# Bucketed attention and two MoE layers on one core: q and k loaded as one transposed tile per head

## The chip, the cores and the metric

The kernel runs on one core of a Trainium2 chip. The metric is device microseconds of one launch, median of 3 runs.

Words used below: TensorE (PE) does matmuls and transposes into PSUM, VectorE (DVE), ScalarE (ACT) and GpSimd (POOL) are the elementwise engines, and SP issues all DMAs of the kernel before. Each engine works through its own instructions in program order and waits at the first one whose inputs or buffers are not ready.

## The reference

There are 2 batches, 8 heads (16 head problems in all), 768 tokens and head dimension 64. All data are float32.

```
q_bits = (q @ proj) > 0 ; k_bits = (k @ proj) > 0        # proj is 64 x 6
bucket = sum(bits * 2**i)                                # 0..63 per token
scores = q @ k.T / 8 ; where(q_bucket != k_bucket, -1e9)
attn   = softmax(scores) (denominator + 1e-9) ; x = attn @ v
x      = heads side by side: 1536 x 512
h = x @ w_in1 ; x = (h * cos(h)) @ w_out1                # 512 -> 2048 -> 512
h = x @ w_in2 ; out = (h * tanh(softplus(h))) @ w_out2
```

## The kernel before

**Precision.** Matmuls run on values rounded to a reduced float32 form (float32r). To keep precision every operand is split into a high part (the rounded value) and a low part (the rest), and a product is the sum of high x high, high x low and low x high.

**Attention.** `attention()` first prepares head 0 in `first_head()`, then runs a loop over t with one *pass* for each block of 128 query rows: six passes (j = 0 to 5) per head. H1 counts the heads in this loop; the scores of head H1 are computed in passes j = 1 to 5 of H1 and j = 0 of the next. A pass issues, in this order: `fin` (U leaves PSUM and is moved to its place), `pt(c, 0)`, `qk(t)`, `exp(t-1)`, `pt(c, 1)`, `pv(c-1)`, then `norm`, a pending addition, one item from a GpSimd list (`gn`) and one piece of weight conversion (`fill`). c is t - 6, so transposing and multiplying with v runs six passes behind the scores. Four slots (0 to 3) inside a pass hold the preparation of the next heads: `plan` says which step goes where; (4, 3) is slot 3 of pass j = 4.

The steps and their names in the profile:

- `qk` (L326, tile s): the scores of 128 queries against 768 keys, two products of 128 contraction rows. Tiles q1 and k1 hold in rows 0 to 63 a one-hot code of the bucket (scaled so that tokens of other buckets fall away) and in rows 64 to 127 the high parts; q2 and k2 hold high and low parts. `s` has two buffers.
- `exp` (L335) writes p and its row sums; `norm` (L344 to L348) scales p by 1/sum, on GpSimd.
- `pt` (L363, wp): three transposes of p blocks; ScalarE copies the high part ph (L367), VectorE the low part pl (L369).
- `pv` (L379, u): four matmuls accumulating into U, which has one PSUM buffer and is copied out by ScalarE in passes j = 2 and 5 (L391, us); a DMA (sh) moves half of it to the other partitions and GpSimd adds both (L396), and every second head splits the result into xh and xl (L399, L402).

Preparing a head (the part that changes): q, k and v are loaded with tokens on partitions (rq, rk, rv, L249). On GpSimd `nat` makes high and low parts side by side (nq, nk, nv; L257, L259), one instruction per pass from the list `gn`. `setup_tr` (L277, wt) transposes three blocks and ScalarE evicts them, for q with the factor 1/8; four such units per head, at (4, 3) and (5, 3) of one head and (0, 1) and (0, 3) of the next. After the second unit of each side a DMA (L279) copies the high rows to q1 or k1. `setup_bits` (L287, wb) is four matmuls per half with proj split high and low, and the sign (L290, sg). `setup_mask` (L294 wm, L300 oh) compares with the 64 codes, and two DMAs (L304, L305) put the one-hot rows into q1 and k1.

The first head does the same steps by hand, with `keep_warm` matmuls (L435, ww) that compute nothing.

**MoE.** `moe()` runs 11 groups of matmuls h (L176) and o (L667) by an order written out in `runs`. While attention runs, four units of weights are already converted in small pieces (`fill`, L131 to L155), from t = 7 on for about eight heads.

Of the kernel before, what the change touches and what calls it, by code (L numbers as in the profile page):

```python
# [25 lines left out]
C_ID, C_CODE, C_SC = 0, 128, 256  # L26
# [3 lines left out]
def host_consts():  # L30
    c = np.zeros((128, NC_CONST), np.float32)
    c[:, C_ID:C_ID + 128] = np.eye(128, dtype=np.float32)
    code = 2.0 * (np.arange(64)[None, :] >> np.arange(6)[:, None] & 1) - 1.0
    c[0:6, C_CODE:C_CODE + 64] = code
    c[32:38, C_CODE + 64:C_CODE + 128] = -code
    c[:64, C_SC], c[64:, C_SC] = -BIG, 1.0
    c[:, C_SC + 1] = np.pi / 2
    c[:, C_SC + 2] = MAGIC
    c[:64, C_SC + 3], c[64:, C_SC + 3] = 5.0, -5.0
    c[:, C_SC + 4] = -1.2e-38  # L40
    c[:, C_SC + 5] = -5.0 * BIG
    return c


@with_exitstack
def lsh_moe_kernel(ctx: ExitStack, tc: tile.TileContext, q, k, v, proj, w_in1, w_out1, w_in2, w_out2, cst, out):
    nc = tc.nc
    B, H, S, D = q.shape
    J = S // 128
    DM = H * D  # L50
# [4 lines left out]
    SCALE = 1.0 / float(D) ** 0.5  # L55
# [18 lines left out]
    oh_s, half_pi, magic, oh_t, tiny, big5 = (con[:, C_SC + i:C_SC + i + 1] for i in range(6))  # L74
    ident_r = persist.tile([128, 128], F32R, name="ident_r")
    pr = persist.tile([128, 6], F32, name="pr")
    prw = persist.tile([128, 2, 128], F32, name="prw")
    prs = persist.tile([128, 2, 2, 128], F32R, name="prs")
# [146 lines left out]
    def attention():  # L225
        actx = ExitStack()
        with actx:
# [12 lines left out]
            NH = B * H  # L240
            rawt, natq, natk, natv = {}, {}, {}, {}
            tt = {}

            srcs = {"q": (q, nat_p, natq, 1), "k": (k, nat_p, natk, 0), "v": (v, v_p, natv, 0)}

            def load(nm, h):
                if h < NH:
                    t = rawt[nm, h] = nat_p.tile([128, J, D], F32, tag="r" + nm, name="r" + nm)
                    nc.sync.dma_start(out=t, in_=srcs[nm][0][h // H, h % H].rearrange("(p j) d -> p j d", j=J))  # L249

            def nat(nm, h):
                if h >= NH:
                    return
                _, pool, dst, hi = srcs[nm]
                r = rawt.pop((nm, h))
                n = dst[h] = pool.tile([128, J, 2, D], F32R, tag="n" + nm, name="n" + nm)
                nc.gpsimd.tensor_scalar(n[:, :, hi, :], r, 1.0, 1.0, ALU.mult, ALU.mult)  # L257
                yield
                nc.gpsimd.tensor_tensor(n[:, :, 1 - hi, :], r, f32(n[:, :, hi, :]), ALU.subtract)  # L259
                yield  # L260

            def tr_unit(n, half):
                w = ps_w.tile([128, HF], F32R, tag="w", name="wt")
                for j in range(3):
                    nc.tensor.transpose(  # L265
                        w[:, j * 128:j * 128 + 128], n[:, 3 * half + j].rearrange("p a d -> p (a d)"), ident_r
                    )
                return f32(w)

            def setup_tr(h, half, side):  # L270
                if half == 0 and side == 0:
                    tt[h] = {nm: t_p.tile([128, S], F32R, tag=nm, name=nm, bufs=2 + (nm[1] == "2")) for nm in ("q1", "q2", "k1", "k2")}
                    tt[h]["oh"] = oh_p.tile([128, S], F32R, tag="oh", name="oh")
                T = tt[h]
                nat_t, a, b, rows, sc = ((natq, "q2", "q1", 64, SCALE), (natk, "k2", "k1", 0, 1.0))[side]
                o = T[a][:, half * HF:half * HF + HF]
                nc.scalar.activation(o, tr_unit(nat_t[h], half), ACTF.Copy, scale=sc)  # L277
                if half == 1:
                    nc.sync.dma_start(out=f32(T[b][64:128, :]), in_=f32(T[a][rows:rows + 64, :]))  # L279
                    nat_t.pop(h)  # L280

            def setup_bits(h, half):
                T = tt[h]
                cs = slice(half * HF, half * HF + HF)
                w = ps_w.tile([128, HF], F32, tag="w", name="wb")
                for i, (x, nm, part) in enumerate((x, nm, part) for x, nm in enumerate(("q2", "k2")) for part in range(2)):
                    nc.tensor.matmul(w, prs[:, part, x, :], T[nm][:, cs], start=(i == 0), stop=(i == 3))  # L287
# [4 lines left out]
            def match(h, half):  # L292
                w = ps_w.tile([128, HF], F32, tag="w", name="wm")
                nc.tensor.matmul(w, code, tt[h]["sg"][:, half * HF:half * HF + HF])  # L294
                return w

            def setup_mask(h, half):
                T = tt[h]
                o = T["oh"]
                nc.vector.tensor_scalar(  # L300
                    o[:, half * HF:half * HF + HF], match(h, half), oh_t, oh_s, ALU.is_gt, ALU.mult
                )
                if half == 1:
                    nc.sync.dma_start(out=f32(T["q1"][0:64, :]), in_=f32(o[0:64, :]))  # L304
                    nc.sync.dma_start(out=f32(T["k1"][0:64, :]), in_=f32(o[64:128, :]))  # L305
# [13 lines left out]
            def qk(t):  # L319
# [4 lines left out]
                for n, (a, c) in enumerate((("q1", "k1"), ("q2", "k2"))[:: 1 if t else -1]):  # L324
# [13 lines left out]
            def norm(t):  # L338
                p, sm = P[t]
                s2 = sm_p.tile([128, 1], F32, tag="s2", name="s2")  # L340
                r = sm_p.tile([128, 1], F32, tag="r", name="r")

                def add():
                    nc.vector.tensor_scalar_add(s2, sm, 1e-9)  # L344

                def scale():
                    nc.vector.reciprocal(r, s2)
# [81 lines left out]
            nc.gpsimd.memset(prw, 0.0)  # L429
# [7 lines left out]
            def first_head():  # L437
                keep_warm(14)
                load("q", 0)
                load("k", 0)  # L440
                nc.sync.dma_start(out=con, in_=cst)
                nc.sync.dma_start(out=pr[0:64, :], in_=proj)
                nc.sync.dma_start(out=pr[64:128, :], in_=proj)
                for nm in "qk":
                    load(nm, 1)
                load("v", 0)
                n = {}
                for nm in "qk":
                    n[nm] = nat_p.tile([128, J, 2, D], F32R, tag="n" + nm, name="n" + nm)
                rq, rk = rawt.pop(("q", 0)), rawt.pop(("k", 0))  # L450
                nc.vector.tensor_copy(n["q"][:, :, 1, :], rq)
                nc.scalar.activation(n["k"][:, :, 0, :], rk, ACTF.Copy)
                nc.vector.tensor_tensor(n["q"][:, :, 0, :], rq, f32(n["q"][:, :, 1, :]), ALU.subtract)
                nc.gpsimd.tensor_copy(ident_r, ident)
                nc.vector.tensor_tensor(n["k"][:, :, 1, :], rk, f32(n["k"][:, :, 0, :]), ALU.subtract)
                nc.gpsimd.tensor_copy(prw[:, 0, 0:6], pr)
                nc.gpsimd.tensor_copy(prw[:, 1, 32:38], pr)
# [3 lines left out]
                T = tt[0] = {  # L461
                    nm: t_p.tile([128, S], F32R, tag=nm, name=nm, bufs=2 + (nm[1] == "2")) for nm in ("q1", "q2", "k1", "k2")
                }
                for half in range(2):
                    cs = slice(half * HF, half * HF + HF)
                    wq, wk = tr_unit(n["q"], half), tr_unit(n["k"], half)
                    nc.scalar.activation(T["q2"][:, cs], wq, ACTF.Copy, scale=SCALE)
                    nc.vector.tensor_copy(T["k2"][:, cs], wk)
                nc.sync.dma_start(out=f32(T["q1"][64:128, :]), in_=f32(T["q2"][64:128, :]))
                nc.sync.dma_start(out=f32(T["k1"][64:128, :]), in_=f32(T["k2"][0:64, :]))  # L470
                for nm in "qk":
                    load(nm, 2)
                for half in range(2):
                    setup_bits(0, half)
                keep_warm(6)
                for half in range(2):
                    cs = slice(half * HF, half * HF + HF)
                    w = match(0, half)
                    nc.scalar.activation(T["q1"][0:64, cs], w[0:64, :], ACTF.Relu, bias=big5[0:64, :], scale=BIG)
                    nc.vector.tensor_scalar(T["k1"][0:64, cs], w[64:128, :], -5.0, -1.0, ALU.is_gt, ALU.mult)  # L480
                load("v", 1)
                for nm, h in (("q", 1), ("k", 1), ("v", 0)):
                    drain(nat(nm, h))
# [34 lines left out]
            for t in range(-1, NT + LAG + 7):  # L518
# [3 lines left out]
                if H1 + 1 < NH:  # L522
                    h = H1 + 1
                    plan.update({
                        (0, 1): lambda: setup_tr(h, 1, 0), (0, 3): lambda: setup_tr(h, 1, 1),
# [207 lines left out]
```

## Time and profile before

| | us |
|---|---|
| median of 3 runs | 784.32 |
| lowest, highest | 783.73, 784.86 |
| profiled execution, span from first to last instruction | 782.2 |
| TensorE busy | 772.9 (99%) |
| VectorE busy | 516.7 (66%) |
| ScalarE busy | 500.9 (64%) |
| GpSimd busy | 221.8 (28%) |

The runs are timed around the launch, the profile from the first to the last instruction, so the time of a run is a little more than a span (2.1 us between the median and the span here). Shares are over the whole span; GpSimd works in the attention stage alone, the first third. The ends of matmuls are modelled, so TensorE's busy share is not its share of peak.

### The profile page before, as it was taken

The numbers are of one execution on the slowest core, as the hardware profiler recorded it, in microseconds if no ns is written. First come the engines' busy times: TensorE is split into PE (matmuls) and PEld (weight loads), VectorE is DVE, ScalarE is ACT, GpSimd is POOL, SyncE is SP. The second block draws the span as 40 slices with busy tenths as digits, with TensorE's granted clock in tenths as the row PEclk, the third lists the DMA queues.
The fourth block names the chain that finished last, engine by engine and source line by source line (L and its number), as shares of the span: only waits on it lengthen the run. The fifth ranks groups of instructions, "written<-read, shape, count | busy, mean of one in ns | idle before, by whom it ended". The sixth has DMA issues, their size and how long they took to land.

```text
span 782.2 us, 11575 instructions
## 1 busy us (share of the span) xinstructions
PE 772.9 (99%) x4020; PEld 662.4 (85%) x4020; DVE 516.7 (66%) x1004; ACT 500.9 (64%) x1002; POOL 221.8 (28%) x267
## 2 busy tenths in 40 slices
PE   8999999999999999999999999999999999999998
PEld 6889999999999788888888888888888888888886
DVE  5899899888997798578876437967213555521122
ACT  5999999998898797677776566955222534322120
POOL 6779999998886300000000000000000000000000
PEclk9999999999999999999999999999999999999999
DMA  5654454434220433113232002333101331000011
GB/s 168 184 149 109 107 147 126 107 99 121 71 67 16 118 109 107 54 54 108 90 99 81 0 1 82 108 108 100 35 1 35 101 106 57 0 23 32 0 54 54
DMA packets 38026, 62.35 MB, mean 80 GB/s; under 512 B 3664, under 2 KB 28368, under 8 KB 37968
## 3 DMA queue, kind: packets, MB, share of 16 engines
q1 hardware_dynamic: 37968, 61.63, 27.1%
q8 instruction: 31, 0.51, 0.3%
q14 instruction: 27, 0.22, 0.1%
HBM read 43.13 MB, written 3.15 MB: 59 GB/s over the span
## 4 chain that ended last, share of the span: by engine, by line
PE 95%; ACT 2%; DVE 1%; issue 1%; DMA 1%; SPq 0%; ACTq 0%
PE o L667 33%; PE h L176 32%; PE u L379 8%; PE s L326 8%; PE wp L363 8%; PE wb L287 3%; PE wt L265 2%; PE s L176 1%; PE wm L294 1%; PE ww L435 1%; DMA k<-oh 1%; DVE pa L643 0%; ACT ph L367 0%; ACT b L195 0%; ACT hs L335 0%
## 5 line engine op out<-in xcount | busy, mean ns | idle before, releaser
L176 PE MATMUL h<-xh,w 128*128 128x512 f32 x752 | 201.0, 389 | 0.0
L211 DVE TENSOR_TENSOR gl<-hs,gh 128x512 fp32r<-128x512 f32 x96 | 66.7, 695 | 192.6 <-ACT gh L209 192.4
L176 PEld LDWEIGHTS h<-xh,w 128*128 128x128 f32 x752 | 141.1, 188 | 29.3
L183 ACT ACTIVATE hs<-h 128x512 f32<-128x512 f32 x48 | 28.7, 598 | 163.2 <-PE h L176 163.2
L369 DVE TENSOR_TENSOR pl<-wp,ph 128x384 fp32r<-128x384 f32 x192 | 105.9, 552 | 23.4 <-ACT ph L367 22.9
L667 PE MATMUL o<-gh,w 128*128 128x512 f32 x384 | 118.3, 389 | 0.0
L667 PE MATMUL o<-w,gh 128*128 128x512 f32 x384 | 118.2, 389 | 0.0
L176 PE MATMUL h<-xl,w 128*128 128x512 f32 x376 | 115.9, 389 | 0.2 <-POOL xl L402 0.2
L367 ACT ACTIVATE ph<-wp 128x384 fp32r<-128x384 f32 x192 | 95.9, 500 | 17.4 <-PE wp L363 17.2
L326 PE MATMUL s<-k,q 128*128 128x512 f32 (+1 forms) x384 | 91.1, 359 | 3.2 <-DVE k L480 0.9
L328 DVE TENSOR_REDUCE nm<-s 128x1 f32<-128x768 f32 x96 | 90.1, 939 | 3.0 <-PE s L326 2.8
L667 PEld LDWEIGHTS o<-w,gh 128*128 128x128 f32 x384 | 72.1, 188 | 15.0
L667 PEld LDWEIGHTS o<-gh,w 128*128 128x128 f32 x384 | 72.0, 188 | 15.0 <-DVE pa L627 0.2
L176 PEld LDWEIGHTS h<-xl,w 128*128 128x128 f32 x376 | 70.5, 188 | 15.2 <-POOL xl L402 0.6
L667 PE MATMUL o<-gl,w 128*128 128x512 f32 x192 | 74.8, 390 | 0.2 <-DVE gl L211 0.2
L667 PE MATMUL o<-w,gl 128*128 128x512 f32 x192 | 74.7, 389 | 0.0
L379 PE MATMUL u<-ph,nv 128*128 128x384 f32 x192 | 72.6, 378 | 0.0
L186 ACT ACTIVATE hs<-h 128x512 f32<-128x512 f32 x46 | 27.5, 597 | 60.4 <-PE h L176 59.6
L326 PEld LDWEIGHTS s<-k,q 128*128 128x128 f32 x384 | 58.3, 189 | 8.5 <-DVE k L480 1.3
L379 PE MATMUL u<-pl,nv 128*128 128x384 f32 x192 | 64.9, 338 | 0.3 <-DVE pl L369 0.3
L209 ACT ACTIVATE gh<-hs 128x512 fp32r<-128x512 f32 x96 | 59.5, 620 | 1.6 <-PE o L667 1.4
L363 PE MATMUL wp<-con,hs 128*128 128x128 f32 x192 | 53.7, 280 | 0.0
(103 smaller groups left out, 1364.1 us busy)
## 6 DMA issues: line engine op xcount, KB each, us to landing
wr<-in_moe_w_in_dram SPq DMA_DIRECT2D x32, 512.0 KB, 3.8
wr<-in_moe_w_out_dram SPq DMA_DIRECT2D x32, 512.0 KB, 3.3
rq<-in_q_dram SPq DMA_DIRECT2D x16, 192.0 KB, 2.8
rk<-in_k_dram SPq DMA_DIRECT2D x16, 192.0 KB, 2.7
rv<-in_v_dram SPq DMA_DIRECT2D x16, 192.0 KB, 3.6
q<-q SPq DMA_DIRECT2D x16, 192.0 KB, 2.7
k<-k SPq DMA_DIRECT2D x16, 192.0 KB, 2.7
sh<-us SPq DMA_DIRECT2D x32, 96.0 KB, 2.3
```

The lines of the kernel that those rows point to most:

```text
L176: nc.tensor.matmul(hp, w[:, wi, c, :], X[b][c], start=(i == 0), stop=(i == 3 * NCT - 1))
L183: nc.scalar.activation(hs, hp, ACTF.Mish)
L186: nc.scalar.activation(hs, hp, ACTF.Copy, scale=INV2PI)
L209: nc.scalar.activation(gh, hs, ACTF.Copy)
L211: nc.vector.tensor_tensor(gl, hs, f32(gh), ALU.subtract)
L326: nc.tensor.matmul(s[:, c0:c1], T[a][:, qs], T[c][:, c0:c1], start=(n == 0), stop=(n == 1))
L328: nc.vector.tensor_reduce(nm, s, AX.X, ALU.max, negate=True)
L363: nc.tensor.transpose(w[:, j * 128:j * 128 + 128], P[h * J + 3 * half + j][:, kt * 128:kt * 128 + 128], ident)
L367: nc.scalar.activation(ph, w, ACTF.Copy)
L369: nc.vector.tensor_tensor(pl, w, f32(ph), ALU.subtract)
L379: nc.tensor.matmul(U[0], lw, x, start=(kt == 0 and n == 0), stop=(kt == J - 1 and n == 1))
L667: nc.tensor.matmul(O[d], lhs, rhs, start=(first and x == 0), stop=(last and x == 2))
```

## The change

The host now lays out, per head, one tile of 128 x 768: rows 0 to 63 are k transposed, rows 64 to 127 q transposed; v is laid out so that each partition reads one run, and proj is padded to 128 x 128 with its columns where the bits of q and k belong. In the kernel:

- one load of 128 x 768 per head takes the place of the loads of q and k; there are three buffers;
- no `nat` for q and k and no transposes. GpSimd multiplies the tile in place by a column that is 1 for k rows and 1/8 for q rows (`setup_scale`), ScalarE copies it to `hi` in one instruction (`setup_high`), GpSimd subtracts in two halves to get `lo` (`setup_low`);
- three DMAs copy k high to k1, q high and q low to q2 (`setup_moves`); after the hash bits one more overwrites the q rows of `lo` with k high, and after the mask two more put the one-hot rows into `hi` and k1. Scores are hi x k1 + q2 x lo;
- the hash bits take three matmuls per half instead of four (hi x proj high, hi x proj low, lo x proj high);
- `first_head` is rewritten, with some loads issued from ScalarE's queue, 10 and 3 instead of 14 and 6 keep_warm matmuls, and two separate code matmuls per half;
- tokens and output rows are in natural order, so output rows are stored in one run; the reciprocal works in place.

The core of the diff:

```diff
+    pw[D:, 0:6], pw[:D, 32:38] = proj, proj
...
+            def load(h):
+                    raw[h] = nat_p.tile([128, S], F32, tag="r", name="r", bufs=3)
+                    nc.sync.dma_start(out=raw[h], in_=kq[h])
...
+            def tiles_of(h):
+                tt[h] = {nm: t_p.tile([128, S], F32R, tag=nm, name=nm, bufs=3) for nm in ("hi", "lo")}
+            def setup_scale(h):
+                if h < NH:
+                    nc.gpsimd.tensor_scalar(raw[h], raw[h], kq_s, 1.0, ALU.mult, ALU.mult)
+            def setup_high(h):
+                nc.scalar.activation(tiles_of(h)["hi"], raw[h], ACTF.Copy)
+            def setup_low(h, half):
+                nc.gpsimd.tensor_tensor(T["lo"][:, cs], raw[h][:, cs], f32(T["hi"])[:, cs], ALU.subtract)
+            def setup_moves(h):
+                for nm in ("k1", "q2"):
+                    T[nm] = t_p.tile([128, S], F32R, tag=nm, name=nm)
+                move(T["k1"][64:128, :], T["hi"][0:64, :])
+                move(T["q2"][0:64, :], T["hi"][64:128, :])
+                move(T["q2"][64:128, :], T["lo"][64:128, :])
+            def bits(h, half):
+                for i, (nm, part) in enumerate((("hi", 0), ("hi", 1), ("lo", 0))):
+                    nc.tensor.matmul(w, prs[:, part, :], T[nm][:, cs], start=(i == 0), stop=(i == 2))
+            def setup_bits(h, half):
+                bits(h, half)
+                if half == 1:
+                    move(T["lo"][64:128, :], T["hi"][0:64, :])
...  # setup_mask, half 1
+                    move(T["hi"][0:64, :], o[0:64, :])
+                    move(T["k1"][0:64, :], o[64:128, :])
...  # qk
+                for n, (a, c) in enumerate((("hi", "k1"), ("q2", "lo"))):
...  # first_head
+                keep_warm(10)
+                nc.sync.dma_start(out=r[:, 0:HF], in_=kq[0, :, 0:HF])
+                nc.scalar.dma_start(out=con[:, 0:C_ID], in_=cst[:, 0:C_ID])
+                nc.sync.dma_start(out=r[:, HF:S], in_=kq[0, :, HF:S])
+                load(1)
+                nc.vector.tensor_scalar(T["hi"][:, 0:HF], r[:, 0:HF], kq_s, 1.0, ALU.mult, ALU.mult)
+                nc.scalar.activation(T["hi"][:, HF:S], r[:, HF:S], ACTF.Identity, scale=kq_s)
+                        T["lo"][:, cs], r[:, cs], kq_s, f32(T["hi"])[:, cs], ALU.mult, ALU.subtract
+                setup_scale(1)
+                setup_moves(0)
+                move(lo2[64:128, :], T["hi"][0:64, :])
+                move(lo2[0:64, :], T["lo"][0:64, :])
+                load_v(0)
+                load(2)
+                load_v(1)
...  # plan: h = H1 + 1, h2 = H1 + 2; the second column is for H1 = 0
+                        (1, 0): lambda: setup_moves(h),
                         (1, 1): lambda: setup_bits(h, 0), (2, 1): lambda: setup_bits(h, 1),
                         (2, 3): lambda: setup_mask(h, 0), (3, 3): lambda: setup_mask(h, 1),
+                        (0, 1): lambda: setup_high(h), (1, 3): lambda: setup_moves(h),
+                    plan[(4, 3)] = lambda: setup_high(h2)
...  # at the end of pass j = 0
+                    if H1:
+                        gn = itertools.chain(lows(H1 + 1, (1,)), nat(H1 + 1), scales(H1 + 2), (None,), lows(H1 + 2, (0,)))
+                    else:
+                        gn = itertools.chain(lows(1, (0, 1)), nat(0), nat(1), scales(2), (None,) * 3, lows(2, (0,)))
+                    load(H1 + 3)
+                    load_v(H1 + 2)
```

`nat` is left for v alone. In H1 = 0 two items of `gn` are issued per pass, later one.

## Rows read from the trace of the kernel before

**Rows 1.** Page, part 1: busy us (share of the span) and instructions of each engine.

```profile
PE 772.9 (99%) x4020; PEld 662.4 (85%) x4020; DVE 516.7 (66%) x1004; ACT 500.9 (64%) x1002; POOL 221.8 (28%) x267
```

**Rows 2.** Page, part 4: the chain that ended last, shares by line.

```profile
PE o L667 33%; PE h L176 32%; PE u L379 8%; PE s L326 8%; PE wp L363 8%; PE wb L287 3%; PE wt L265 2%; PE s L176 1%; PE wm L294 1%; PE ww L435 1%; DMA k<-oh 1%; DVE pa L643 0%; ACT ph L367 0%; ACT b L195 0%; ACT hs L335 0%
```

**Rows 3.** Windows: length, busy us (instructions) per engine, TensorE clock, DMA share, GB/s.

```profile
54.12:84.17 30.05, 30.05 (x213) 28.29 (x213) 28.04 (x67) 28.29 (x67) 28.62 (x34) 1.00 0.46 123
...
144.45:174.60 30.15, 30.15 (x214) 28.50 (x213) 26.70 (x65) 27.44 (x65) 27.78 (x34) 1.00 0.39 106
174.60:204.81 30.21, 30.21 (x215) 28.60 (x213) 26.65 (x64) 27.50 (x66) 26.58 (x33) 1.00 0.41 106
```

**Rows 4.** Chain of waits, 54 to 85 us: start, us, engine, tile, line, count.

```profile
60.84 0.18 PE wm L294
...
69.29 0.70 PE wb L287 x4
...
76.01 0.18 PE wm L294
...
78.25 0.21 PE wt L265 x3
...
79.84 0.70 PE u L379 x4
...
84.33 0.71 PE wb L287 x4
```

**Rows 5.** Groups by shape: line, engine, out<-in, count | busy us, mean ns | idle before.

```profile
L335 ACT ACTIVATE hs<-s,nm 128x768 f32<-128x768 f32 x32 | 29.2, 912 | 1.3 <-DVE nm L328 1.3
...
L348 POOL TENSOR_SCALAR hs<-hs,r 128x768 f32<-128x768 f32 x32 | 30.3, 948 | 12.3 <-DVE r L347 4.8 <-PE u L379 3.8 <-ACT p L335 1.3
...
L277 ACT ACTIVATE q<-wt 128x384 fp32r<-128x384 f32 x30 | 15.4, 515 | 1.9 <-PE wt L265 0.4
```

**Rows 6.** Timeline of GpSimd, 60 to 92 us: start, us, instruction.

```profile
62.64 1.00 POOL L259 TENSOR_TENSOR nk<-rk,nk 128x384 fp32r<-128x384 f32 x1
...
71.39 0.51 POOL L257 TENSOR_SCALAR nq<-rq 128x384 fp32r<-128x384 f32 x1
...
78.40 1.01 POOL L259 TENSOR_TENSOR nk<-rk,nk 128x384 fp32r<-128x384 f32 x1
```

**Rows 7.** Timeline of ScalarE, 76 to 80 us, around the eviction of pass j = 4.

```profile
77.88 0.49 ACT L367 ACTIVATE ph<-wp 128x384 fp32r<-128x384 f32 x1
78.49 0.49 ACT L277 ACTIVATE q<-wt 128x384 fp32r<-128x384 f32 x1
78.88 0.49 ACT L391 ACTIVATE us<-u 128x384 f32<-128x384 f32 x1
```

**Rows 8.** Timeline of GpSimd, 180 to 212 us: items of pass j = 3.

```profile
183.37 1.01 POOL L259 TENSOR_TENSOR nk<-rk,nk 128x384 fp32r<-128x384 f32 x1
...
198.19 1.02 POOL L259 TENSOR_TENSOR nk<-rk,nk 128x384 fp32r<-128x384 f32 x1
```

**Rows 9.** DMA issues: out<-in, queue, count, KB each, median us to landing.

```profile
wr<-in_moe_w_in_dram SPq DMA_DIRECT2D x32, 512.0 KB, 3.8
...
q<-q SPq DMA_DIRECT2D x16, 192.0 KB, 2.7
...
k<-oh SPq DMA_DIRECT2D x15, 192.0 KB, 3.0
```

**Rows 10.** Chain of waits, 0 to 24 us.

```profile
1.12 4.28 PE ww L435 x14
...
8.26 0.99 PE ww L435 x6
...
11.17 0.62 PE s L326 x2
...
18.11 4.07 DMA k<-oh
...
22.32 0.94 PE s L326 x4
```

**Rows 11.** Timeline of VectorE, 0 to 5 us: its first work on loaded data.

```profile
3.13 0.36 DVE L451 CAST nq<-rq 128x384 fp32r<-128x384 f32 x1 [2.06 <-DMA rq<-in_q_dram]
```

More of the change, by code (lines that the diff above doesn't have):

```diff
@@ L41, in host_consts, with lay_out, lsh_moe_kernel @@
     c[:, C_SC + 5] = -5.0 * BIG
+    c[:64, C_SC + 6], c[64:, C_SC + 6] = 1.0, 0.125
     return c
+def lay_out(inputs):
+    q, k, v, proj = (np.asarray(inputs[n]) for n in ("q", "k", "v", "proj"))
+    B, H, S, D = q.shape
+    kq = np.concatenate([x.reshape(B * H, S, D).transpose(0, 2, 1) for x in (k, q)], axis=1)
+    vt = v.reshape(B * H, S // 128, 128, D).transpose(0, 2, 1, 3).reshape(B * H, 128, -1)
+    pw = np.zeros((2 * D, 128), np.float32)
+    pw[D:, 0:6], pw[:D, 32:38] = proj, proj
+    return {"kq": kq, "v": vt, "proj": pw}
 @with_exitstack
-def lsh_moe_kernel(ctx: ExitStack, tc: tile.TileContext, q, k, v, proj, w_in1, w_out1, w_in2, w_out2, cst, out):
+def lsh_moe_kernel(ctx: ExitStack, tc: tile.TileContext, kq, v, proj, w_in1, w_out1, w_in2, w_out2, cst, out):
     nc = tc.nc
-    B, H, S, D = q.shape
+    NH, _, S = kq.shape
+    D = proj.shape[0] // 2
     J = S // 128
-    DM = H * D
+    DM = w_in1.shape[0]
+    H = DM // D
+    B = NH // H
     NCT = DM // 128
@@ L73, in lsh_moe_kernel @@
     ident = con[:, C_ID:C_ID + 128]
[L74 to L78, printed above, removed]
+    oh_s, half_pi, magic, oh_t, tiny, big5, kq_s = (con[:, C_SC + i:C_SC + i + 1] for i in range(7))
+    prw = persist.tile([128, 128], F32, name="prw")
+    prs = persist.tile([128, 2, 128], F32R, name="prs")
     code = persist.tile([128, 128], F32R, name="code")
@@ L258, in nat @@
                 yield
-                nc.gpsimd.tensor_tensor(n[:, :, 1 - hi, :], r, f32(n[:, :, hi, :]), ALU.subtract)
+                nc.gpsimd.tensor_tensor(n[:, :, 1, :], r, f32(n[:, :, 0, :]), ALU.subtract)
                 yield
[L262 to L273, printed above, removed]
-                T = tt[h]
[L275 to L280, printed above, removed]
@@ new lines, in scales, with lows @@
+            def scales(h):
+                setup_scale(h)
+                yield
+            def setup_high(h):
+                nc.scalar.activation(tiles_of(h)["hi"], raw[h], ACTF.Copy)
+            def setup_low(h, half):
+                T, cs = tt[h], half_of(half)
+                nc.gpsimd.tensor_tensor(T["lo"][:, cs], raw[h][:, cs], f32(T["hi"])[:, cs], ALU.subtract)
+            def lows(h, halves):
+                for half in halves:
+                    if h < NH:
+                        setup_low(h, half)
+                    yield
@@ new lines, in move @@
+            def move(dst, src):
+                nc.sync.dma_start(out=f32(dst), in_=f32(src))
+            def setup_moves(h):
+                T = tt[h]
+                raw.pop(h)
+                for nm in ("k1", "q2"):
[4 more added lines that the diff above has]
+            def bits(h, half):
+                T, cs = tt[h], half_of(half)
@@ L437, in first_head @@
             def first_head():
[L438 to L456, printed above, removed]
@@ L469, in first_head @@
[L469 to L472, printed above, removed]
-                for half in range(2):
[L474 to L480, printed above, removed]
@@ L481, in first_head @@
-                load("v", 1)
-                for nm, h in (("q", 1), ("k", 1), ("v", 0)):
-                    drain(nat(nm, h))
+                T = tiles_of(0)
+                nc.vector.tensor_scalar(T["hi"][:, 0:HF], r[:, 0:HF], kq_s, 1.0, ALU.mult, ALU.mult)
+                nc.scalar.activation(T["hi"][:, HF:S], r[:, HF:S], ACTF.Identity, scale=kq_s)
+                for half in range(2):
+                    cs = half_of(half)
+                    nc.vector.scalar_tensor_tensor(
+                        T["lo"][:, cs], r[:, cs], kq_s, f32(T["hi"])[:, cs], ALU.mult, ALU.subtract
+                    )
@@ new lines, in first_head @@
+                nc.gpsimd.tensor_copy(code, con[:, C_CODE:C_CODE + 128])
+                setup_scale(1)
+                setup_moves(0)
+                lo2 = t_p.tile([128, S], F32R, tag="lo", name="lo", bufs=3)
+                move(lo2[64:128, :], T["hi"][0:64, :])
[3 more added lines that the diff above has]
+                load_v(1)
+                for half in range(2):
+                    bits(0, half)
+                T["lo"] = lo2
@@ L485, in early @@
+                keep_warm(3)
+                ws = [[match(0, 0), match(0, 0)], [match(0, 1), match(0, 1, ps_u, "u")]]
+                for half in range(2):
+                    cs, (wq, wk) = half_of(half), ws[half]
+                    nc.vector.tensor_scalar(T["k1"][0:64, cs], wk[64:128, :], -5.0, -1.0, ALU.is_gt, ALU.mult)
+                    nc.scalar.activation(T["hi"][0:64, cs], wq[0:64, :], ACTF.Relu, bias=big5[0:64, :], scale=BIG)
             def early():
@@ L563, in attention @@
                 if j == 0:
-                    gn = itertools.chain(nat("q", H1 + 2), nat("k", H1 + 2), nat("v", H1 + 1))
-                    for nm in "qk":
-                        load(nm, H1 + 3)
-                    load("v", H1 + 2)
+                    if H1:
[4 more added lines that the diff above has]
+                    load_v(H1 + 2)
                 if 0 <= t - 1 < NT:
@@ L574, in attention @@
                     later.pop(0)[1]()
-                next(gn, None)
+                for _ in range(1 if H1 else 2):
+                    next(gn, None)
                 if 3 <= t < 6:
@@ L719 @@
     arrays, args = {}, []
-    ins = [(n, _np.ascontiguousarray(inputs[n])) for n in _INS]
+    laid = lay_out(inputs)
+    ins = [(n, _np.ascontiguousarray(laid.get(n, inputs.get(n)))) for n in _INS]
     ins = [(n, a.view(_np.int64) if a.dtype == _np.float64 else a) for n, a in ins] + [("consts", host_consts())]
```

77 lines of the change are left out of this document (30 added, 47 removed).

## The prediction

> **What bounds the kernel now.** I read the engine totals first: TensorE is busy for 99% of the span [rows 1]. The chain of waits by line agrees: nearly all of it is matmul lines, and the lines that the change touches are small, 2.8% for the hash bits (wb) and 1.6% for the transposes (wt) [rows 2]. Two thirds of the chain (h and o) is the MoE stage, whose matmuls the change leaves alone. So all that can move lies in the attention stage, the first 250 us or so.
>
> There the windows matter. One window of two heads is 30.05 us: TensorE busy for all of it, but GpSimd 28.62, ScalarE 28.29 and VectorE 28.04 [rows 3]. Later pairs have more air (GpSimd 27.78, then 26.58). A head lasts 84.33 - 69.29 = 15.04 us by the chain, with TensorE back to back [rows 4]. So each microsecond taken from TensorE is real, but three engines stand within 2 us per pair behind it.
>
> **The change part by part.** *TensorE.* A head loses four wt groups at 0.21 us and two of its eight wb matmuls, at 0.70/4 each [rows 4]: 0.84 + 0.35 = 1.19 us. That happens in 14 heads (H1 = 1 to 14; head 0 is bound by latency, head 15 prepares nothing): 16.7 us if all of it shows.
>
> *GpSimd.* It loses the nq and nk pairs, 2 x (0.51 + 1.01) [rows 6], and gains one in-place scaling of 128x768, the shape and kind of the row-normalizing L348 at 0.95 [rows 5], and two lo halves of 128x384, subtractions like nk at 1.01: 3.04 against 2.97, say 0.1 us less a head. In the first three steady pairs (H1 = 3 to 8, where the weight pieces run) it needs 28.62 - 0.2 = 28.4 us, more than the 27.67 that TensorE then needs (30.05 - 2.38). There the floor is GpSimd: at most 1.6 us a pair.
>
> *ScalarE.* Four evictions of 0.515 go, one copy of 128x768 comes [rows 5]; no row has that shape from SBUF, so I bound it by two 384 evictions (1.0) and one Exp of 768 (0.91) from above, one eviction (0.5) from below, and take 0.8. ScalarE gains over 1 us a head, but its place matters. In the pass j=4 it now does the copy to hi, and before that must wait for GpSimd's scaling, issued at the end of j=3. The next thing in its queue is the copy us of U, and TensorE's first pv matmul of j=5 may start only after that, since U has one buffer. Before, in head H1=4: the eviction q starts at 78.49, us at 78.88, done at 79.37, and pv starts at 79.84 [rows 4, 7]. The cover is under 0.5 us.
>
> Now the walk. In head H1=4 TensorE ends j=3 at 76.01 + 0.18 = 76.19 and GpSimd starts its item of that pass at 78.40, 2.2 us late; in H1=3, which has no queue behind it, the two are at 60.84 + 0.18 and 62.64, 1.6 us apart [rows 4, 6]. Unloaded: scaling done 1.6 + 0.9 = 2.5 us after the end of j=3, copy and us done 0.72 + 0.49 later, 3.7; pv wants to start 79.84 - 76.19 - 0.21 (the wt gone) = 3.44. TensorE stalls about 0.3 us, so such a head gains 1.19 - 0.3 = 0.9. Loaded: from one j=3 item to the next GpSimd worked 15.76 us nearly without a break (62.64 to 78.40), 15.7 after the change; the scaling is done 1.6 + 15.7 + 0.9 = 18.2 us after the end of the earlier j=3, while TensorE reaches its own end of j=3 after 76.19 - 61.02 - 1.19 + 0.3 = 14.3. That is 3.9 late, less some 0.2 for a stall at the hash bits, which now wait for the second lo half: us done at 4.9, stall 1.5. So 0.3 + 0.2 + 1.5 = 2.0 of the pair's 2.38 goes again and 0.4 stays. The walk lets GpSimd gain nothing from the stalls, and the floor says 1.6: I take 0.7 a pair, nearer the walk. In the fifth pair the interval is 198.19 - 183.37 = 14.82 [rows 8]; the same walk gives stalls of 0.3 and 0.8 and a gain of 1.3; the fourth pair lies between, 1.0. The sixth (H1=13, 14) gains 0.9 + 1.19, because head 14 makes no copy.
>
> *SP and the moves.* Four moves a head become six, and three stand in series: q2 from lo, then lo from hi (it overwrites what the first reads), then hi from the mask. They land in 2.7 us, the last k1 move in 3.0 [rows 9]. From the second lo half (GpSimd, 71.39 + 1.0 in the old order [rows 6]) to the next head's first scores (84.33 - 0.70) are 11.2 us, 10.0 after the change; needed are 2.7 + 2.7 + 0.5 + 3.0 and some waking, 9.1. It is covered, by 0.9 us. Queued behind them at SP are the sh moves and the loads; their readers come one pass or one head later, so I cost them at nothing.
>
> The Trainium skill, "DMA: Bandwidth & Descriptors", section "Two DMAs through the same engine are not ordered", says that a transfer depending on an earlier one must wait for its completion semaphore, sharing a queue being no substitute; the profile of before has no move that depends on another move, so no row shows it. Were queue order enough, the start below would gain 4 us more.
>
> *The start.* First scores wait for the masks until 11.17 [rows 10]. The new order drops two rounds of transposes and evictions, but queues five moves (0.5 us of SP each) of which the mask in hi must wait for the fourth: before, work on the first load began at 3.13 [rows 11]; half a load later, with conversions of some 0.5, hi is done near 4.2 and lo near 5.3, the fourth move is issued at 5.8 and landed at 8.5, ScalarE writes the mask, and scores begin at 9.1: an estimate, 2 us earlier. Head 1 loses that: its copy follows at 9.5 to 10.3, two lo halves to 12.3, and SP stands at the load of v for head 2 until GpSimd has split v of head 0, 13.8; then load, three moves (the third issued 15.3), landings 18.0, 20.7 and, for k1 behind the mask, 24.0. Before, head 1's scores began at 22.32 [rows 10]. I take +1.7 us; bounds -2.3 (no series) and +4 (landing 4.07, as beside the weight loads, and a TensorE that after idling issues at the pace of the first warm matmuls, 4.28/14 = 0.31 us, against 0.99/6 = 0.165 [rows 10]).
>
> *The rest:* heads 1 and 2 follow the unloaded figure (2 x 0.9); natural row order of v and out, fewer constants and the in-place reciprocal change no count on the path and stand at nothing, 0.3 us either way.
>
> **Sum.** Start +1.7, heads 1 and 2 -1.8, three loaded pairs -2.1, fourth -1.0, fifth -1.3, sixth -2.1: -6.6 us on an execution whose span is 782.2, so 775.6; the runs' median is 784.32, 2.1 more for what lies around the span, so 777.7.
>
> **The rivals.** (B) TensorE stays the bound: lags shrink since ScalarE is freer. For it: TensorE never paused from 69 to 84 us [rows 4]; against: the cover of 0.47 us before pv. Start -2.3, three pairs at the floor -4.8, eight other heads -9.5: -16.6, 767.7. (C) The stalls take nearly all: every head keeps only the 0.2 us that the walk leaves in a loaded pair, 14 x 0.2 = 2.8, and the start costs 1.7 to 4: 783.2 to 785.5. For it: between its items at 183.37 and 198.19 [rows 8] GpSimd has the same queue of x splits; against: light pairs have 1 to 2 us less for GpSimd [rows 3]. (D) Slower: the three moves decide. Their spare is 0.9 us in all, so it decides once the mean landing passes 3.1 us. If they land in 3.8 us as the weight loads do [rows 9], the chain is 12.1, 2.1 late; in ten of 14 heads that is +21 against -16.7, and with the start's +1.7 the time is about 790. Against it: six 192 KB moves a head are a light load where the DMA share is 0.46 [rows 3]. That the change doesn't do what it says would be the copy or scaling landing on the path at full length; that is C.
>
> **How the numbers follow.** Forecast (772 to 782.5) 0.42; B (764 to 772) 0.26; C 0.17; D 0.15. 0.2% of 784.32 is 1.6 us, about what can be told from no change. Faster: forecast and B, 0.68; same: C, 0.17; slower: D, 0.15. The range leaves a tenth at either end: below 766 only a full B, above 788 a full D.
>
> **What would show it.** Right: no wt group, six wb matmuls a head; heads near 14.2 us where light and near 14.7 where weight pieces run; ScalarE idle before the hi copy released by GpSimd's scaling; TensorE's wait at u released by us; head 1's scores near 24 us released by a DMA. B: heads of 13.85 with no TensorE wait. D: TensorE waiting on DMA k1 or hi at every head's first scores. The forecast is wrong if the hi copy never waits, or if GpSimd's lag at j=3 shrinks below 1.2 us.

## The result: slower by 0.9%, and the profile after

The changed kernel took 791.78 us (median of 4 runs, 791.6 to 792.1) against 784.41 us in the same comparison: ratio 1.0093, 95% interval [1.0081, 1.0106]. The forecast was 777.7 us, the range 766 to 788. The profiled execution took 791.6 us, its span is 789.8.

Page of the changed kernel, part 1, the clock row of part 2 (40 slices) and the chain by engine:

```profile
PE 764.7 (97%) x3791; PEld 645.4 (82%) x3791; DVE 513.5 (65%) x1002; ACT 488.8 (62%) x955; POOL 220.1 (28%) x248
...
PEclk9799999999999999999999999999999999999999
...
PE 84%; DVE 6%; POOL 3%; ACT 2%; DMA 2%; issue 1%; SPq 0%; ACTq 0%; POOLq 0%
```

Against [rows 1]: 229 matmuls fewer and 8.2 us less of TensorE; yet the span grew by 7.6, so TensorE stands still for some 16 us more. The clock row has one low slice, the second (20 to 40 us). To find where the time goes I read the start of the first hash matmul (wb) of each head in TensorE's timeline of both kernels:

| stretch (first wb of head H1) | before | after | difference | predicted |
|---|---|---|---|---|
| start to H1=1 | 23.09 | 30.14 | +7.05 | +1.7 |
| H1=1 to 3 | 30.86 | 31.36 | +0.50 | -1.8 |
| H1=3 to 9 (weight pieces run) | 90.65 | 92.11 | +1.46 | -2.1 |
| H1=9 to 14 | 75.26 | 74.24 | -1.02 | -3.2 |
| H1=14 to the end | | | -0.4 | -1.2 |

The marks at H1=1, before and after:

```profile
23.09 0.52 PE L287 MATMUL wb<-q,prs 128*128 128x384 f32 x2
```
```profile
30.14 0.84 PE L319 MATMUL wb<-hi,prs 128*128 128x384 f32 x2
```

The hash bits of head 1, below, are those at H1=1 in this table (they prepare head 2); moves are counted by the head that they prepare.

Two losses, then: most at the start, the rest spread over the heads. The start, chain of waits of the changed kernel (start, us, what):

```profile
1.17 3.06 DMA r<-in_kq_dram
...
4.31 1.28 ACT L487
5.60 0.62 ACT hi L487
...
8.09 3.54 DMA lo<-hi
...
12.27 0.56 ACT hi L510
12.83 0.74 ACT hi L291
...
13.65 1.97 POOL lo L295 x2
...
17.76 1.00 POOL nv L272
...
25.54 3.05 DMA k<-oh
...
28.73 1.62 PE s L364 x4
```

The SP queue's own timeline over the same stretch and into the next head (start, us of issuing, line):

```profile
17.22 0.33 SPq L263 DMA_DIRECT2D rv<-in_v_dram  x1
...
18.81 0.59 SPq L304 DMA_DIRECT2D q<-lo  x1
22.33 0.46 SPq L304 DMA_DIRECT2D lo<-hi  x1
25.03 0.46 SPq L304 DMA_DIRECT2D hi<-oh  x1
25.54 0.59 SPq L304 DMA_DIRECT2D k<-oh  x1
26.18 1.20 SPq L131 DMA_DIRECT2D wr<-in_moe_w_in_dram  x2
...
30.46 0.55 SPq L304 DMA_DIRECT2D q<-lo  x1
39.70 0.46 SPq L304 DMA_DIRECT2D lo<-hi  x1
42.39 0.46 SPq L304 DMA_DIRECT2D hi<-oh  x1
42.90 0.59 SPq L304 DMA_DIRECT2D k<-oh  x1
```

Read the gaps between q<-lo and lo<-hi: 3.5 us in head 1, but 9.2 in head 2, with three weight loads of 512 KB (and head 4's 384 KB and head 3's 192 KB) issued on the queue just before; run 9 takes the weight loads away. Head 1's first scores come at 28.73 (before: 22.32 [rows 10]), and head 2's first hash bits 9.06 us later than before, of which 7.05 are there at H1=1 already.

The steady heads, windows of the changed kernel (columns as in [rows 3]); two pairs with weight pieces and a light one:

```profile
61.50:92.21 30.71, 29.37 (x187) 25.72 (x186) 27.99 (x68) 27.00 (x62) 28.61 (x32) 1.00 0.58 156
92.21:122.91 30.70, 29.33 (x187) 25.64 (x186) 27.98 (x68) 26.98 (x62) 28.62 (x32) 1.00 0.53 136
153.61:183.28 29.67, 28.54 (x186) 25.96 (x185) 26.10 (x65) 25.72 (x60) 27.58 (x32) 1.00 0.48 131
```

The kernel before, from the same marks (H1=3 to 5, H1=9 to 11):

```profile
53.95:84.17 30.22, 30.22 (x215) 28.46 (x214) 28.12 (x67) 28.46 (x68) 28.79 (x34) 1.00 0.46 123
144.60:174.71 30.11, 30.11 (x215) 28.50 (x213) 26.66 (x64) 27.40 (x66) 27.74 (x34) 1.00 0.39 106
```

The windows of [rows 3] begin off these marks (54.12 is one matmul late, 174.60 is 0.11 early), so a loaded pair before is 30.22 us, not 30.05, and a light one 30.11. No engine fills its pair now: TensorE waits 1.1 to 1.4 us in each. The waits say for what (engine, line, releaser: us in all, times, longest):

```profile
ACT hi L291 <- POOL r L284: 7.4, 13, 1.2
PE u L416 <- ACT us L428: 6.2, 12, 0.8
PE s L364 <- DMA k<-oh: 6.2, 2, 4.6
```

And one instance in three timelines, GpSimd, ScalarE and TensorE:

```profile
70.20 0.91 POOL L284 TENSOR_SCALAR r<-r,con 128x768 f32<-128x768 f32 x1
```
```profile
71.14 0.84 ACT L291 ACTIVATE hi<-r 128x768 fp32r<-128x768 f32 x1 [0.71 <-POOL r L284]
71.89 0.47 ACT L428 ACTIVATE us<-u 128x384 f32<-128x384 f32 x1
```
```profile
72.41 0.44 PE L416 MATMUL u<-ph,nv 128*128 128x384 f32 x1 [0.75 <-ACT us L428]
```

Scaling, hi copy, us, pv: the very chain that was forecast. The last row of the waits settles rival D: TensorE waits for the serial moves in two heads (1 and 2), not in all. The time is close to the 790 that D gave, but by luck: the waits in ten heads from which D got it aren't there.

### The profile page after: what moved, and what is told of

It is laid out like the page before. It is cut to its first block, busy times and chain, and to the rows that moved or that the text cites. A ratio compares the mean times of both kernels' runs of the same rounds, so it can differ in the third digit from the quotient of the medians.

```text
span 789.8 us, 10982 instructions
## 1 busy us (share of the span) xinstructions
PE 764.7 (97%) x3791; PEld 645.4 (82%) x3791; DVE 513.5 (65%) x1002; ACT 488.8 (62%) x955; POOL 220.1 (28%) x248
## 4 chain that ended last, share of the span: by engine, by line
PE 84%; DVE 6%; POOL 3%; ACT 2%; DMA 2%; issue 1%; SPq 0%; ACTq 0%; POOLq 0%
PE o L696 33%; PE h L188 32%; PE u L416 6%; PE s L364 5%; PE wp L400 5%; DVE pl L406 2%; DVE nm L366 2%; PE wb L319 1%; DMA k<-oh 1%; DMA lo<-hi 1%; ACT us L428 1%; POOL r L284 1%; ACT ph L404 1%; PE s L188 1%; POOL hs L385 1%
## 5 line engine op out<-in xcount | busy, mean ns | idle before, releaser
L404 ACT ACTIVATE ph<-wp 128x384 fp32r<-128x384 f32 x192 | 93.2, 495 | 24.4 <-PE wp L400 24.0
L364 PE MATMUL s<-k,hi 128*128 128x512 f32 x192 | 58.5, 387 | 11.6 <-DMA k<-oh 6.2
L364 PE MATMUL s<-lo,q 128*128 128x512 f32 x192 | 50.6, 346 | 0.0
```

Source lines behind the costliest of these rows:

```text
L364: nc.tensor.matmul(s[:, c0:c1], T[a][:, qs], T[c][:, c0:c1], start=(n == 0), stop=(n == 1))
L404: nc.scalar.activation(ph, w, ACTF.Copy)
```

## The experiments

Each undoes or moves one suspected cost in the changed kernel. Ratios, with their 95% intervals, are against the kernel before in the same comparison (the changed kernel has 1.0093); a difference without a ratio is against the changed kernel's 791.78 us. Several of these kernels scatter more than the changed one (0.5 us); where a trace is of an execution far from the median, the text says so.

**1. The scaling ahead of the split of v in GpSimd's queue.**

```diff
-gn = itertools.chain(lows(H1 + 1, (1,)), nat(H1 + 1), scales(H1 + 2), (None,), lows(H1 + 2, (0,)))
+gn = itertools.chain(lows(H1 + 1, (1,)), scales(H1 + 2), nat(H1 + 1), (None,), lows(H1 + 2, (0,)))
```

> The changed kernel with one edit: GpSimd's scaling for head H1+2 is issued at the end of pass j=1 instead of j=3, and the split of v after it. Theory A (in each head ScalarE's copy to hi waits for GpSimd's scaling, the copy of U behind it starts late, and TensorE's pv of j=5 waits): ScalarE's wait for the scaling (7.4 us in 13 heads) goes, light heads go from 14.85 to about 14.3 us and loaded ones from 15.35 to about 14.9, in all some 6.5 us: 785. Rival B (the total work of GpSimd and VectorE is the limit in each head, the place of the scaling doesn't matter): at most 1.5 us, 790 to 792.

787.18 us (786.0 to 789.4, the trace is of the lowest), ratio to the kernel before 1.0039 [1.0026, 1.0052]: 4.6 us back, of the 6.5 that theory A gave and more than the rival's 1.5. The page's waits no longer have u behind us; the windows of two pairs with pieces and a light one:

```profile
61.91:91.35 29.44, 29.28 (x186) 25.90 (x185) 27.51 (x66) 26.43 (x61) 28.44 (x32) 1.00 0.58 160
91.35:121.19 29.84, 29.59 (x186) 25.92 (x185) 28.33 (x70) 27.05 (x62) 29.02 (x32) 1.00 0.55 142
...
150.61:179.25 28.64, 28.64 (x186) 25.93 (x185) 26.21 (x65) 25.63 (x60) 27.53 (x32) 1.00 0.51 135
```

So the stall cost about 1.0 us a pair (0.9 to 1.3), loaded or light. In the loaded pairs GpSimd is now busy for 97% (28.44 of 29.44, 29.02 of 29.84), close to the floor of the prediction, which shows only once the stall is gone. The chains point the same way. Shares by line in a loaded stretch, first of the changed kernel (73 to 85 us), then of this run (72 to 90 us):

```profile
by line: DVE pl L406 38.9%; DVE nm L366 35.7%; DVE cg L157 9.0%; DVE ct L154 6.3%; DVE oh L340 4.9%; DVE r L384 3.5%; DVE ct L152 2.8%; DVE r L381 2.0%; issue 0.1%
```
```profile
by line: PE u L416 27.4%; PE wp L400 22.5%; PE s L364 22.1%; POOL lo L295 10.9%; POOL hs L385 6.5%; POOL xl L439 4.1%; PE wb L319 2.5%; POOL xh L436 2.1%; PE wm L332 1.9%; issue 0.9%; POOLq L433 0.1%
```

With the stall VectorE's lines fill the chain of these 12 us (over 72 to 90 us they make two thirds, TensorE's and ScalarE's the rest); without it TensorE and GpSimd share the chain and VectorE is gone from it. In the light pair of this run the chain is TensorE's alone. That GpSimd sets the loaded pairs is read from these shares; no run takes work from GpSimd. The start is unchanged (scores at 28.76).

**2. Three v buffers**, so that SP's load of v no longer waits for GpSimd's split of head 0.

```diff
-rawv[h] = nat_p.tile([128, J, D], F32, tag="rv", name="rv")
+rawv[h] = nat_p.tile([128, J, D], F32, tag="rv", name="rv", bufs=3)
```

> The changed kernel with a third buffer for the raw v tile, so that SP no longer stands at the load of v for head 2 until GpSimd has split v of head 0 (4.0 us in the profile). Theory S1 (the start is a chain through this load): head 1's three moves are issued about 1.6 us earlier (first at 15.7 instead of 17.65), head 1's scores begin near 27 instead of 28.7, and the time falls by 1.5 to 2 us: 790. Rival (the scores wait for the mask and for the moves of the mask whatever comes before): no change, 791.8.

789.19 us, 1.0065 [1.0048, 1.0082], 2.6 us back; head 1's scores at 25.25, 3.5 us earlier. The SP wait was real, more than the 1.5 to 2 us expected, and worth somewhat less at the end than at its place.

**3. A tile of its own for the swapped lo rows**: five of seven moves go in one burst ahead of the hash bits, the two of the mask follow as before. The lo tile gets two buffers instead of three.

```diff
 ...
+T["lk"] = t_p.tile([128, S], F32R, tag="lk", name="lk")
+move(T["lk"][64:128, :], T["hi"][0:64, :])
 ...
+move(T["lk"][0:64, :], T["lo"][0:64, :])
 ...
-if half == 1:
-    move(T["lo"][64:128, :], T["hi"][0:64, :])
 ...
```

> The changed kernel with the series of dependent moves broken: the second product reads a tile of its own (lk), filled by two moves of k low and k high right after the others, instead of overwriting the q rows of lo; seven moves a head instead of six. Theory S2 (the series costs only at the start, where nothing covers it): head 1's scores begin at 23 to 24 us instead of 28.7, TensorE idles less and keeps its clock, the steady heads stay at 15.35 and 14.85 us: 783 to 786. Rival D (the series decides in each head): steady heads fall by 0.5 to 1 us too, 775 or less. Rival (a seventh move crowds the queue): steady heads grow, over 788.

797.51 us (792.8 to 799.8, the trace is of the highest), 1.016 [1.012, 1.02]: a miss, 5.7 us worse. Head 1 did gain (scores at 24.39 instead of 28.73, head 2's hash bits at 40.24 instead of 46.93), and it was all lost later: in the trace the three loaded pairs take 101.48 us instead of 92.11. The chain of head 2's moves, and the waits:

```profile
21.99 5.98 DMA wr<-in_moe_w_in_dram
...
27.99 6.37 DMA lk<-lo
```
```profile
POOL xt L434 <- DMA sh<-us: 13.9, 5, 6.7
ACT hi L291 <- POOL r L284: 13.7, 12, 2.7
PE u L417 <- ACT us L429: 13.4, 12, 2.5
```

The burst of five moves stands ahead of the sh move on the queue; GpSimd's x addition waits for sh (13.9 us against 7.3 in the changed kernel), the scaling queued behind it comes late, and the stall at u doubles (13.4 against 6.2 us). The two lo buffers are no likely cause: run 7 has them too and loses nothing. The prediction cost what is queued behind the moves at nothing; with one move more it isn't.

**4. The fourth hash matmul back.**

```diff
-enumerate((("hi", 0), ("hi", 1), ("lo", 0)))
+enumerate((("hi", 0), ("hi", 1), ("lo", 0), ("lo", 1)))
```

> The changed kernel with the fourth hash-bit matmul of each half put back (lo times the low part of proj): 0.175 us more TensorE work twice in 15 heads, 5.2 us. Theory A (TensorE waits for others in every head): the time grows by 0 to 1.5 us, 792 to 793. Rival P (TensorE is still the bound, the loss is all in the start): +5 us, 797.

794.16 us, 1.0126 [1.011, 1.0141]: 2.4 us for some 5.2 us of matmuls, between the theories. In the trace 1.3 us of it is there by H1=3; from H1=3 to 14 the heads lengthen by 1.3 us for 11 x 0.35 = 3.9 us of matmuls. So there about a third of what TensorE saves shows and waits take up the rest; the wait for us accounts for 1.0 of that (5.2 us here against 6.2), the others were not taken apart.

**5. Warm matmuls in the two idle stretches of the start**, to hold the clock.

```diff
+if half == 0:
+    keep_warm(20)
 ...
+if t == J:
+    wu = ps_u.tile([128, HF], F32, tag="u", name="wu")
+    for _ in range(24):
+        nc.tensor.matmul(wu, warm[:, 0:128], warm)
```

> The changed kernel with matmuls on a constant tile put where TensorE idles in the first head: 20 after the first code matmuls, 24 ahead of head 1's first scores; nothing else. Theory C (the idle stretches of 4 to 5 us lower TensorE's clock, granted 0.50 at 25 to 30 us and 0.68 at 30 to 35, and the work after them runs at half pace, head 1's matmuls from 28.7 to 33.4 us): the clock stays at 1.0, head 1's first scores begin no earlier, but its hash bits of pass j=2 come 2 us earlier: 789 to 790. Rival (the work there waits for other engines anyway): no change, 791.5 to 792.5.

793.65 us (791.8, 792.0, 795.3 and 796.5, the trace is of the last), 1.0127 [1.0099, 1.0155]: no gain, and the 1.9 us of the median are within the scatter. The clock did hold (1.00 in 30 to 35 us), and head 1's second hash half came 1.8 us earlier (31.63); but head 2's bits came at 48.52 instead of 46.93: they wait for k<-oh, which the matmuls' pace doesn't move and which landed after 4.01 us here instead of 3.16. Behind that wait the clock fell after all, one head later (granted 0.63 in 45 to 50 us and 0.69 in 50 to 55, where the changed kernel has 1.00). So the low clock moved, and what it costs in the changed kernel this run can't tell.

**6. A one-column ScalarE copy ahead of the data**, which takes the 1.28 us ahead of hi.

```diff
+pre = sm_p.tile([128, 1], F32, tag="pre", name="pre", bufs=1)
 ...
+nc.vector.memset(pre, 0.0)
+nc.scalar.activation(pre, pre, ACTF.Copy)
```

> The changed kernel with a one-column copy on ScalarE ahead of its first conversion, so that the table load (1.28 us, now behind the first data, 4.31 to 5.59) runs while the data are on their way. Theory S3 (the table load is on the chain of the start): hi of the second half, the moves and head 1's scores come 1.2 us earlier: 790.5. Rival (the start is bound by GpSimd and SP later): no change, 791.8.

790.67 us, 1.0096 [1.0076, 1.0116]: 1.1 us back by the median (three runs at 790.6 to 790.7, one at 794.0), but the interval holds the changed kernel's ratio, so the time alone doesn't show it. The trace does for the start: hi starts at 4.27 instead of 5.60, head 1's scores at 27.36 instead of 28.73. The Trainium skill, "ScalarE: Activation LUTs", section "What ACT_TABLE_LOAD costs", gives 1283 ns for loading the table of another set of functions; the 1.28 us row agrees. The same sentence adds about 1380 ns of drain, which does not show here: hi starts 0.01 us after the row ends.

**7, 8. Parts together:** the scaling moved, three v buffers and the own lo tile (7); the scaling moved, three v buffers, warm matmuls and the early copy (8).

> Early scaling, the third raw v buffer and the broken series together. Alone they gave -4.6, -2.6 and +5.7 us. Theory A/S (the seventh move hurts because the sh move waits behind the burst, GpSimd's addition behind sh, and the scaling behind the addition; with the scaling issued ahead of that addition the hurt goes and the start's gain of 4.5 us at head 1's scores stays): 779 to 783. Rival (seven moves crowd the DMA queues whatever stands behind them): 788 or more.

> Early scaling, the third raw v buffer, the constant matmuls and the early table load together, six moves a head. If the parts add up (-4.6, -2.6, about -2, about -1.2): 781 to 782, faster than the kernel before. Rival (they hide one another: at the start one chain after the other shows up): 785 to 787.

Run 7: 783.0 us, 0.9985 [0.9973, 0.9996], just faster than before, at the upper end of theory A/S. With the scaling early, the own tile costs no stall at u, though GpSimd's x addition still waits 10.9 us for sh (7.3 in the changed kernel). Run 8: 784.2 us, 1.0002 [0.9992, 1.0013], 2 to 3 us short of what was expected: k<-oh, issued at 21.27, had landed by 26.2 (4.9 us), and the 24 warm matmuls stood in the scores' way for 1.7 us more. Its chain:

```profile
22.31 5.58 PE wu L583 x24
27.89 0.69 PE s L364 x4
```

**9. The three weight loads later** (and their pieces), the changed kernel otherwise.

```diff
-if 3 <= t < 6:
+if 14 <= t < 17:
     load_w()
-if t >= 7:
+if t >= 18:
     fill(j)
```

> The changed kernel with the three first expert weight loads issued at steps t = 14 to 16 instead of 3 to 5, and the conversion pieces from t = 18 instead of 7; nothing else. Theory W (head 2's moves are stretched by the 512 KB weight loads on the same queue: q<-lo 8.6 us from issue to landing, lo<-hi issued at 39.70 only): q<-lo lands in 3 to 4 us, head 2's hash bits (wb at H1=2) come at 41 to 43 instead of 46.93, and the time falls by 3 to 5 us, to 787 to 789. Rival X (head 2 is late because head 1 was, the loads only fill a wait): wb at H1=2 stays within 1.5 us of 46.93 and the time within 1 us of 791.8.

794.31 us, 1.0125 [1.011, 1.0141]: 2.5 us worse, a miss in time. Head 2's q<-lo landed after 5.64 us instead of 9.19, and no wait for k<-oh is left there; but its bits came at 45.53, only 1.4 us earlier and not at 41 to 43. So most of head 2's lateness was head 1's, as rival X has it. Head 3 paid (17.28 us instead of 15.05). Chain:

```profile
56.93 6.31 DMA sh<-us
63.38 0.99 POOL xt L433
64.45 0.99 POOL lo L295
65.49 0.46 PE wb L319
```

The sh move behind the three loads took 6.31 us where 96 KB mostly take 2.5 in this run: the place moved, the cost stayed. A second cost came with it: the pieces now run until 191 us instead of 159, so the pair from H1=9 is a loaded one and takes 30.69 us instead of 29.67. Runs 10 to 12 start the pieces as late.

**10, 11. The gains with the late loads** (10: scaling, v buffers, early copy; 11: also the own lo tile in head 1 alone).

```diff
+T["lk"] = T["lo"]
+if h == 1:
+    T["lk"] = t_p.tile([128, S], F32R, tag="lk", name="lk", bufs=1)
 ...
-if half == 1:
+if half == 1 and h != 1:
     move(T["lo"][64:128, :], T["hi"][0:64, :])
```

> Scaling ahead of the v split, three v buffers, the table loaded early, and the weight loads and pieces late, all in one. If the start and the stalls before the hi copy are the whole loss, the gains of single runs (4.6, 2.6, 1.1 us) add to theory W's 3 to 5: 779 to 781, faster than before (784.4) by 0.4 to 0.7%. If the loads do nothing (X): 783 to 784, no difference from before. If the parts take each other's place as three of them did with the warm matmuls: 784 to 785.

> As the run before it, with a tile of its own for the swapped lo rows in head 1 alone, so that head 1's moves go in one burst ahead of the hash bits; the other heads keep the serial move after the bits. If head 1's chain of moves still sets its scores: they start at 23 to 24 instead of about 25 and the time falls by another 1 us, to 778 to 780. If head 2's own chain sets what follows: head 2's wb within 0.5 us of the run before, and the same time.

784.6 us (781.8 to 787.3), 1.0005 [0.9993, 1.0017], and 782.0 us (780.8 to 783.7, the trace is of the highest), 0.9969 [0.9958, 0.998]; both fall short of what was expected. Run 10's is what the single runs add up to (791.8 - 4.6 - 2.6 - 1.1 + 2.5 = 786.0) and 1.4 less, which is within its scatter. Run 11's hash bits: H1=1 at 24.25, 2 at 37.81, 3 at 52.00; the kernel before has 23.09, 37.87, 53.95, so the start's loss is gone by head 2. Then head 3 takes 18.6 us, behind the same burst (sh 6.27 us). The own tile in one head brings 2.6 us without run 3's price.

**12. As 11, one weight load a head.**

```diff
-if 14 <= t < 17:
+if t in (10, 16, 22):
```

> As the run with head 1's own lo tile, but the three weight loads are issued one per head (steps t = 10, 16 and 22) instead of three in a row (t = 14, 15, 16); pieces from t = 18 as there. There, head 3 lasts 18.6 us (hash bits at 52.0, next at 70.6), since sh<-us took 6.3 us behind the loads and GpSimd's x addition and the second lo half waited for it. Theory L (the burst on the shared queue makes that head long): hash bits of H1=3 at 52 again, of H1=4 at 67 to 68, and the time falls by 3 to 5 us to 777 to 779, faster than before by 0.7 to 0.9%. Rival M (each single load holds the moves or sh behind it just as long, so three heads lose 1 to 1.5 us each instead of one losing 4): 781 to 782.5, no gain over that run. Rival N (the loss in head 3 is the start of the pieces themselves): H1=4 at 70 or later and 782.

778.52 us (778.3 to 779.5), 0.9931 [0.9917, 0.9945] against before: theory L. H1=3 at 51.71, H1=4 at 66.22 (run 11: 70.60). This version beats both kernels. Head 1's scores start at 23.26. A stretch of about a pair with pieces still has GpSimd busy for 97%:

```profile
66.90:96.50 29.60, 29.44 (x187) 26.07 (x186) 28.09 (x69) 26.87 (x62) 28.79 (x32) 1.00 0.58 159
```

By the hash marks the pairs from H1=5 and H1=7 last 30.14 and 30.64 us, longer than in run 1, so more than GpSimd's work still costs time there.

## Why the prediction was wrong

**The step that failed first: "The start ... I take +1.7 us".** It measured +6.41 at head 1's first scores and +7.05 at its hash bits, 5.35 of the 14.2 us by which the sum missed. The steps of its walk were the right ones, in the right order; their times were not. By scores of head 0, 3.3 us were lost: "hi is done near 4.2" was 6.22, since the load landed only at 4.24 (work began at 3.13 before [rows 11]) and 1.28 us of ScalarE came ahead of the first activation (run 6); the fourth move was put at 2.7 us and took 3.54, and the mask's second half ended at 12.83. The rest: "SP stands at the load of v ... 13.8" was 17.2 (run 2: worth 3.5 us at head 1's scores), and three moves in series took 3.5, 2.7 and 3.05 (runs 3 and 11 take the series away in head 1). The bound of +4 was too near because it charged each landing and the clock, but no delay of the walk's first item. The 0.64 between scores and bits lies in a stretch at 0.50 granted clock: the group of scores takes 1.41 us there, before 0.77. What the low clock adds behind that stays open (run 5).

**Heads 1 and 2, -1.8 predicted, +0.5 measured.** "Heads 1 and 2 follow the unloaded figure" failed: by the time head 2's moves are issued, weight loads fill the queue. Its q<-lo landed 9.2 us after its issue, 6.5 more than the 2.7 assumed, against a spare of 0.9 for the whole series. With the weight loads later (run 9) the same stretch, H1=1 to 3, took 29.77 us instead of 31.36, so they make 1.6 of the 2.3 us missed; the other 0.7 no run took apart. Spread over three heads (run 12, whose head 1 also has its own lo tile) it took 27.68. That is rival D's mechanism in one head: it was weighed as a mean over all heads and never looked for beside the weight loads.

**Loaded pairs, 0.7 us gain each predicted, 0.5 us loss measured** (30.70 against 30.22). The walk and the floor were treated as two answers, with a value between them, and the step that failed is this choice: in the runs they add. The walk's stall of 1.8 us a pair (0.3 and 1.5) was too large: it is 0.9 to 1.3 (run 1). But without it a pair lasts 29.42 to 29.84 at GpSimd 97% busy, where the prediction had 27.67 for TensorE alone and 28.4 for the floor, so 1.0 to 1.4 us stood in no term of the sum. Of that, 0.8 to 1.0 is GpSimd standing idle between its items; what for, no run took apart.

**Light pairs: -1.0 and -1.3 predicted, -0.4 and -0.3 measured; the sixth, -2.1 predicted, about -0.7.** The mechanism held to the instruction: scaling, copy (0.84 against 0.8 taken), us, pv. Its size was off: 0.3 us of stall a head was predicted in the light heads, and run 1 gives (29.67 - 28.64)/2 = 0.5 for it. A further 0.45 a head is left in run 1 (28.64 against 30.11 - 2.38 = 27.73), where the page counts TensorE busy throughout. More than half of it lies at the transposes of p: from one start to the next TensorE takes 0.092 us there, before 0.085 (72 a pair). Why stays open, and so does the 0.8 us by which the last stretch fell short (H1=14 to the end).

**What was right.** The saving on TensorE is real: the wt groups are gone, a wb group takes 0.53 us for 0.70, and a light pair without the stall is 1.47 us shorter (28.64 against 30.11), three fifths of the 2.38 counted; run 4 loses when one matmul comes back. That "three stand in series" was right too. The Trainium skill, "DMA: Bandwidth & Descriptors", section "Two DMAs through the same engine are not ordered", was cited there for a dependent move having to wait for the landing of the one before; no row of before showed it. The changed kernel's SP does wait so, 2.6 us a head; whether queue order would have done, no run tries:

```profile
SPq L304 <- DMA q<-lo: 39.6, 15, 8.6
...
SPq L304 <- DMA lo<-hi: 31.8, 15, 3.0
```

With several of these costs taken out (run 12) the time falls by 5.8 us, close to the 6.6 that was forecast. That nearness is luck: by the stretches of the table run 12 has +0.9, -3.2, -0.4, -2.4 and -0.5, where the sum had +1.7, -1.8, -2.1, -3.2 and -1.2, and it gains at the start by edits that the sum doesn't hold.

## What to carry to other kernels

A move that waits for another move is priced by the worst neighbour on its queue, not by its median: look up what else is issued there in the heads where it first runs. When work is taken from the bound engine, walk the next engine's queue at the place where its new item must be ready, and move that item up before anything else; that one line was worth 4.6 us here. A floor and a stall found by two different walks of the same stretch are not two bounds with the truth between them: here both showed, and the pair grew. And two kernels' windows are compared from the same mark, since one matmul off was 0.17 us of the 0.5 in question here.

## What the runs showed of the hardware that was not expected

In and after the idle stretch of 4.6 us ahead of head 1's scores TensorE had the lower clock, 0.50 granted (1.2 GHz) in 25 to 30 us and 0.68 on average in 30 to 35, windows of the changed kernel:

```profile
25.00:30.00 5.00, 1.27 (x4) 1.11 (x5) 0.35 (x2) 0.60 (x2) 1.52 (x3) 0.50 0.71 187
30.00:35.00 5.00, 5.00 (x25) 4.73 (x24) 3.06 (x6) 3.27 (x7) 1.06 (x2) 0.68 1.02 326
35.00:40.00 5.00, 5.00 (x35) 4.71 (x35) 4.83 (x12) 4.36 (x11) 3.02 (x4) 1.00 0.64 120
```

Fully busy in both, it made 25 matmuls in the second of these windows and 35 in the third. With the first idle stretch filled (run 5) the low clock came one head later, behind the next one. And the landing of one and the same kind of move, q<-lo of 192 KB, went from a median of 3.1 us to 9.2 behind three 512 KB loads.
